# Linear attention and a mixer in one kernel: a new table of ranks and a new order of loads for its planner

## Chip, cores and metric

One core of one Trainium2 chip. The metric is the device time of one execution in microseconds (us). The program computes in fp32 and in pairs of fp32r halves.

## The reference, cut to what matters

```python
# q, k, v: (4, 4, 1088, 32); S1, S2: (8, 32)
def phi(x):                                   # 64 features of a row
    a = einsum('rd,bhsd->bhsr', S1, x)
    b = einsum('rd,bhsd->bhsr', S2, x)
    return einsum('bhsi,bhsj->bhsij', a, b).reshape(*x.shape[:-1], 64)
q_p, k_p = phi(q), phi(k)
kv  = einsum('bhsf,bhsd->bhfd', k_p, v)
z   = sum(k_p, axis=2)
num = einsum('bhsf,bhfd->bhsd', q_p, kv)
den = einsum('bhsf,bhf->bhs', q_p, z)[..., None] + 1e-06
x   = num / den                               # then (4, 1088, 128)
h   = maximum(x.transpose(0, 2, 1) @ w_tok1, 0) @ w_tok2      # 1088 -> 256 -> 1088
u   = x + h.transpose(0, 2, 1)
out = u + maximum(u @ w_ch1, 0) @ w_ch2                       # 128 -> 1536 -> 128
```

The weights arrive as 64-bit floats.

## The kernel before

The work goes batch by batch (b = 0 to 3). For each batch: the features of the keys (`keys`: L534 projects, L564 multiplies, L581 sums them with the values into `kv`, and L591 copies `kv` into the image `kvz`, step `K0.kvz` for batch 0); the features of the queries (for batch 0 on TensorE, L672; for the others `Q1.p` and so on, L727, whose result L736 copies and DMAs turn); then `mixing`: the attention (L790, steps `A0.x0` to `x2`), the denominators (L798) and the division (L806 and L808, steps `A0.d0` to `d2`), token mixing in three groups (L846 for batch 0, L852 for the others, steps `A0.t0` to `t2`), relu, a transpose (L886), the second token matrix (L968, L972) on top of the residual (L877, steps `A0.u0` to `u2`), and the split of the sum into two halves (L943, L946). `channel_mix` takes the columns in spans of 384 (two of 320, one of 256 at the end): for each of 12 slices of the 1536 channels three matmuls L1022 into `ps_h` (steps `.f`), the relu half L1026 on ScalarE (`.h`), the rest L1029 on VectorE (`.l`), and three matmuls L1035 into `ps_o` (`.s`). For the three spans of batch 0 the slices interleave: slices 0 to 2 of the first and of the second span, 3 to 5 of both, 6 to 11 of both, then the third.

A weight piece wi (w = 0, 1 token matrices, 2, 3 channel matrices; "14" is piece 4 of matrix 1) is loaded as doubles and converted by `convert`: `abs` (L384) and `low` (L388) on ScalarE, `clamp` (L391), `shift` (L395, into a `ps_h` bank) and `merge` (L398) on VectorE, `add` (L405, L407) on GpSimd; then `hi` (L504) on ScalarE and `lo` (L507) split it. Pieces 00 to 03 and all of matrices 2 and 3 have 512 columns, 04 has 256, 10 to 13 have 384, 14 and 15 have 320; at 128 partitions and 8 bytes that is 512, 256, 384 and 320 KB (of 1,024 bytes). One batch of keys is 576 KB, of queries 544, of values 594. Of batch 0, the first four key tiles (256 KB) go over ScalarE's queue and k0 is the other 320 KB; q0a is 192 KB and q0b 352.

The program is not written out in its order. Each step is an `Op` with a cost on each engine that may do it, and `Plan.run` places them one by one: of all ready steps it takes those that can start first by its own costs, and of these the one with the highest rank. The rank is the longest chain of costs behind the step plus an offset from the table `LEAD` (in the planner's ns; steps of one name share it). An offset beyond some hundred thousand puts a step before or behind all others that are ready with it. `LOADS` is the order of the loads in SP's queue. Buffers are few: three PSUM banks `ps_a`, three `ps_h`, two `ps_o`; four buffers `c` and four `tail` for conversions. In its own clock the planner keeps VectorE's `port=True` steps and all GpSimd steps from overlapping. Where TensorE would stand idle, `fill` puts matmuls on the identity (L362).

```python
for op in self.ops:
    op.level += op.boost + LEAD.get(op.name, 0.0)
...
first = min(b[0] for b in best)
near = [b for b in best if b[0] <= first]
top = max(near, key=lambda b: b[3].level + STICK * (b[2] == "pe" and b[3].mode == mode))
```

Of the kernel before, what the change touches and what calls it, by code (L numbers as in the profile page):

```python
# [32 lines left out]
PAD = 64  # L33
CUTS = {0: (2, 2, 2, 2, 1), 2: (4, 4, 4), 3: (4, 4, 4)}
SIZES = ([n * DTOK for n in CUTS[0]], [cn for _, cn in CHUNKS for _ in range(2)], [n * P for n in CUTS[2]], [n * P for n in CUTS[3]])
LOADS = "k0 q0a 00 v0 q0b 01 02 03 04 10 k1 11 12 13 q1 20 32 30 21 v1 31 15 22 14".split()


WIDE = 384
# [2 lines left out]
def _spans():  # L42
# [22 lines left out]
KEYS_ON_POOL = set()  # L65

LEAD = {
    "A0.d1": -168600.0,
    "A0.d2": -1620100.0,
    "A0.t2": -90600.0,  # L70
    "A0.u0": -461300.0,
    "A0.u1": 126500.0,
    "A0.ul00": 26500.0,
    "A1.n1": 207400.0,
    "A1.xT0": -108100.0,
    "A2.h0": -154900.0,
    "A2.n0": 210600.0,
    "A2.w1": -3726400.0,
    "A2.w2": -80800.0,
    "A2.x": -16100.0,  # L80
    "A2.xb": -788400.0,
    "A3.n0": 775400.0,
    "A3.n1": 210300.0,
    "A3.w1": 89200.0,
    "A3.w2": 127600.0,
    "K0.kvz": -2428600.0,
    "K1.c0": 982200.0,
    "K1.kvz": -2006700.0,
    "K1.s": -439400.0,
    "K1.v0": 26700.0,  # L90
    "K1.v4": -1229500.0,
    "K2.p": 5500.0,
    "K2.s": 631300.0,
    "K3.p": 645000.0,
    "Q0.a20": 606400.0,
    "Q0.m20": -56700.0,
    "Q0.p1": 183300.0,
    "Q1.r00": 75800.0,
    "Q1.r01": 221700.0,
    "Q1.r11": -287800.0,  # L100
    "Q3.p": -1564300.0,
    "U0.l": -3600.0,
    "U0.s": -888200.0,
    "U1.ol": 570300.0,
    "U1.s": -310000.0,
    "U10.s": -2000.0,
    "U11.s": -1400.0,
    "U2.f": 181200.0,
    "U2.h": -146700.0,
    "U2.s": -764700.0,  # L110
    "U3.f": 8400.0,
    "U3.s": 5700.0,
    "U4.f": 762600.0,
    "U4.h": 68000.0,
    "U6.s": -230900.0,
    "U8.f": 192500.0,
    "U8.s": -591000.0,
    "U9.f": -390200.0,
    "U9.h": 261700.0,
    "s.low": 6600.0,  # L120
    "s.rows": 95400.0,
    "w00.clamp": -462300.0,
    "w00.lo": -3161100.0,
    "w01.abs": 311700.0,
    "w01.hi": -124600.0,
    "w01.lo": -2636700.0,
    "w02.abs": 28200.0,
    "w02.hi": -455000.0,
    "w02.lo": -4313300.0,
    "w02.low": -1051800.0,  # L130
    "w02.shift": 141200.0,
    "w03.clamp": 120200.0,
    "w03.hi": -107500.0,
    "w03.lo": -2645500.0,
    "w03.shift": -1556200.0,
    "w04.hi": -2453000.0,
    "w04.lo": -2852800.0,
    "w10.abs": -1284500.0,
    "w10.clamp": 69000.0,
    "w11.clamp": 246000.0,  # L140
    "w11.hi": -1243300.0,
    "w11.lo": -134000.0,
    "w11.low": 448400.0,
    "w11.merge": -659300.0,
    "w12.abs": 99900.0,
    "w12.hi": 475400.0,
    "w12.low": -24500.0,
    "w12.merge": -269500.0,
    "w13.hi": -300400.0,
    "w13.merge": -144100.0,  # L150
    "w13.shift": -1219700.0,
    "w14.abs": -2780200.0,
    "w14.clamp": 192400.0,
    "w15.abs": -4153500.0,
    "w15.clamp": 149200.0,
    "w20.clamp": -574900.0,
    "w20.low": -1570500.0,
    "w21.low": 310000.0,
    "w22.abs": -997600.0,
    "w22.low": -1298000.0,  # L160
    "w32.abs": -2006300.0,
    "w32.low": -2863700.0,
}


# [154 lines left out]
def attn_mixer_kernel(ctx: ExitStack, tc: tile.TileContext, qT, kT, v1, s64, wt1, wt2, wc1, wc2, out):  # L320
# [143 lines left out]
    by_kind = {"q": (load_q, q_loaded), "k": (load_k, k_loaded), "v": (load_v, v_loaded)}  # L464
    for name in LOADS:
        if name[:2] == "q0":
# [45 lines left out]

    for name in LOADS:
        if name[0].isdigit():
# [566 lines left out]
    for b in range(B):  # L1081
# [3 lines left out]
        if not b:  # L1085

            for name in LOADS:
                if name[0] in "01":
# [58 lines left out]
```

## Time and profile before

| | us |
|---|---|
| median of 3 runs | 220.97 (220.74 to 222.49) |
| the profiled execution | 220.62 |
| its span | 218.7 |
| TensorE's matmuls busy | 211.2 |
| VectorE, ScalarE, GpSimd busy | 137.7, 117.3, 80.3 |

The span runs from the first to the last instruction of the program in the trace. PE is TensorE's matmul, PEld its weight load, DVE VectorE, ACT ScalarE, POOL GpSimd, SP the queue of DMAs. Matmuls are pipelined: their listed durations overlap, so a group's length is read from its start to the next start.

### The profile page before, as it was taken

The page shows a single profiled execution, that of the slowest core. Times are in us where ns is not written, and L with a number is a line of the kernel's source. Part 1 is how long each engine was busy: PE and PEld are TensorE (multiplying, and loading weights), DVE is VectorE, ACT ScalarE, POOL GpSimd, SP SyncE. Part 2 cuts the span into 40 slices and gives each one's busy share as a digit, 9 for nine tenths or more (in the row PEclk, how much of TensorE's full clock was granted, in tenths as well). Part 3 has the DMA queues.
Part 4 walks back from the last instruction along what each step waited for, and adds up shares of the span by engine and source line. Part 5 has one row for each costly group of instructions (what it writes and reads, how often), then busy time and mean ns, then how long its engine had stood idle before and what let it go on. Part 6 is the DMA issues. An engine that isn't in the chain of part 4 may idle for free.

```text
span 218.7 us, 4927 instructions
## 1 busy us (share of the span) xinstructions
PE 211.2 (97%) x1884; PEld 199.4 (91%) x1884; DVE 137.7 (63%) x276; ACT 117.3 (54%) x283; POOL 80.3 (37%) x87
## 2 busy tenths in 40 slices
PE   7997999998999999999999999999999999999994
PEld 7766679997998999999999999999999999999993
DVE  2887999879759456555833455568137655556562
ACT  4588799994545324543532544455226544355551
POOL 3165597989899102740500220745003200000000
PEclk9999999999999999999999999999999999999998
DMA  6999996994106589610250258400510000100000
GB/s 194 390 410 407 406 393 205 186 211 151 37 3 226 128 223 155 172 66 3 85 170 0 74 142 146 174 0 27 191 38 1 3 36 0 36 3 36 0 30 27
DMA packets 11399, 28.36 MB, mean 130 GB/s; under 512 B 1520, under 2 KB 5616, under 8 KB 11376
## 3 DMA queue, kind: packets, MB, share of 16 engines
q1 hardware_dynamic: 11232, 27.79, 41.3%
q8 instruction: 15, 0.25, 0.5%
q10 hardware_dynamic: 144, 0.26, 0.4%
q14 instruction: 8, 0.07, 0.1%
HBM read 23.21 MB, written 4.83 MB: 128 GB/s over the span
## 4 chain that ended last, share of the span: by engine, by line
PE 83%; DMA 11%; DVE 1%; SPq 1%; issue 1%; ACT 0%
PE ps_h L1022 33%; PE ps_o L1035 32%; DMA doubles<-wt 11%; PE ps_a L852 4%; PE ps_a L972 4%; PE ps_a L790 3%; PE ps_a L581 3%; PE ps_a L968 1%; PE ps_a L534 1%; SPq L366 1%; PE ps_a L727 1%; DVE k_p L564 1%; PE ps_a L877 0%; PE ps_a L886 0%; DVE hl L1029 0%
## 5 line engine op out<-in xcount | busy, mean ns | idle before, releaser
L1029 DVE SCALAR_TENSOR_TENSOR hl<-ps_h,hh 128x384 fp32r<-128x384 f32 (+2 forms) x144 | 74.9, 532 | 54.9 <-ACT hh L1026 54.5
L1026 ACT ACTIVATE hh<-ps_h 128x384 fp32r<-128x384 f32 (+2 forms) x144 | 67.8, 477 | 58.7 <-PE ps_o L1035 36.2
L1022 PE MATMUL ps_h<-uh,halves 128*128 128x384 f32 (+2 forms) x288 | 88.1, 334 | 0.9 <-DVE hl L1029 0.9
L1035 PE MATMUL ps_o<-hh,halves 128*128 128x384 f32 (+2 forms) x288 | 70.6, 327 | 0.0
L1022 PEld LDWEIGHTS ps_h<-uh,halves 128*128 128x128 f32 x288 | 53.3, 188 | 4.0 <-DVE hl L1029 2.7
L1035 PEld LDWEIGHTS ps_o<-hh,halves 128*128 128x128 f32 x288 | 50.3, 188 | 0.0
L1022 PE MATMUL ps_h<-ul,halves 128*128 128x384 f32 (+2 forms) x144 | 47.0, 327 | 0.0
L1035 PE MATMUL ps_o<-hl,halves 128*128 128x384 f32 (+2 forms) x144 | 47.0, 327 | 0.0
L1022 PEld LDWEIGHTS ps_h<-ul,halves 128*128 128x128 f32 x144 | 27.1, 188 | 0.2
L1035 PEld LDWEIGHTS ps_o<-hl,halves 128*128 128x128 f32 x144 | 27.0, 188 | 0.0
L946 POOL TENSOR_TENSOR ul<-us,uh 128x64 fp32r<-128x64 f32 (+4 forms) x15 | 9.6, 656 | 46.5 <-ACT uh L943 46.3
L770 POOL TENSOR_TENSOR qp<-qp,br 128x544 f32<-128x544 f32 x12 | 16.2, 1367 | 13.2 <-PE ps_o L1035 9.7
L818 POOL TENSOR_TENSOR xl<-x,xh 128x384 fp32r<-128x384 f32 x9 | 8.9, 1014 | 13.5 <-ACT xh L814 8.5
L564 DVE TENSOR_TENSOR k_p<-ps_a,a_sb 128x1024 f32<-128x1024 f32 (+1 forms) x12 | 11.0, 948 | 4.3 <-ACT a_sb L544 4.3
L405 POOL TENSOR_TENSOR whole<-c,tail 128x512 int32<-128x512 int32 (+3 forms) x11 | 11.7, 1071 | 3.3 <-ACT abT L736 2.0
L384 ACT ACTIVATE c<-doubles 128x512 f32<-128x512 f32 (+3 forms) x17 | 10.7, 628 | 3.2 <-DMA doubles<-wt 2.2
L507 POOL TENSOR_TENSOR halves<-whole,halves 128x384 fp32r<-128x384 f32 (+3 forms) x11 | 11.5, 1062 | 0.0
L790 PEld LDWEIGHTS ps_a<-kvz,qp 128*64 128x64 f32 x288 | 8.8, 138 | 2.5 <-ACT kvz L591 1.3
L790 PE MATMUL ps_a<-kvz,qp 128*64 128x66 f32 x288 | 9.5, 224 | 1.4 <-ACT kvz L591 1.1
L388 ACT ACTIVATE tail<-doubles 128x512 int32<-128x512 uint32 (+3 forms) x17 | 10.5, 624 | 0.0
L395 DVE TENSOR_SCALAR ps_h<-c 128x512 int32<-128x512 int32 (+3 forms) x17 | 10.3, 617 | 0.1
L398 DVE SCALAR_TENSOR_TENSOR c<-doubles,ps_h 128x512 int32<-128x512 int32 (+3 forms) x17 | 10.3, 609 | 0.1
(78 smaller groups left out, 229.0 us busy)
## 6 DMA issues: line engine op xcount, KB each, us to landing
qp<-rows SPq DMA_DIRECT2D x6, 544.0 KB
br<-rows SPq DMA_DIRECT2D x12, 272.0 KB
doubles<-wc SPq DMA_DIRECT2D x6, 512.0 KB
v_sb<-v SPq DMA_DIRECT2D x4, 594.0 KB
doubles<-wt SPq DMA_DIRECT2D x4, 512.0 KB
k_sb<-kT SPq DMA_DIRECT2D x3, 576.0 KB
xm<-xb SPq DMA_DIRECT2D x3, 576.0 KB
xT<-xm SPq DMA_DIRECT2D x12, 144.0 KB
```

Of the source, the lines that this page charges most:

```text
L384: nc.scalar.activation(f32(t["c"]), f32(high), AF.Abs)
L388: nc.scalar.activation(t["tail"], low.bitcast(U32), AF.Copy, scale=2.0 ** -29)
L395: nc.vector.tensor_scalar(t["ps"], t["c"], 3, 0x3FFFFFFF, op0=ALU.logical_shift_left, op1=ALU.bitwise_and)
L405: engines[e].tensor_tensor(dst(), t["c"], t["tail"], op=ALU.add)
L507: engines[e].tensor_tensor(halves[w, i][:, 1], f32(whole[w, i] if w < 2 else t["c"]), f32(halves[w, i][:, 0]), op=ALU.subtract)
L564: engines["pool" if on_pool else "dve"].tensor_tensor(t["k_p"][:pn, t0 * H:t1 * H], a.unsqueeze(3).broadcast_to([pn, n, R, R]), t["sb", t0 ...
L770: engines[e].tensor_tensor(qp[:, p, cs], qp[:, p, cs], t["br"][:, p, cs], op=ALU.mult)
L790: nc.tensor.matmul(x_ps[c:c + 64, o:o + 2 * (D + 1)], lhsT=qp[:, p, s0 + c:s0 + c + 64], rhs=kvz_all[b % 2][:, p, :2 * (D + 1)], start=Tru ...
L1022: nc.tensor.matmul(h_ps[:, :cn], lhsT=part(2, at[2][e][0], l, at[2][e][1] * P, P), rhs=r[:, :cn], start=(m == 0), stop=(m == 2))
L1026: nc.scalar.activation(t["hh"][:, :cn], t["h"][:, :cn], AF.Relu)
L1029: nc.vector.scalar_tensor_tensor(t["hl"][:, :cn], t["h"][:, :cn], 0.0, f32(t["hh"][:, :cn]), op0=ALU.max, op1=ALU.subtract)
L1035: nc.tensor.matmul(outs[i][:, :cn], lhsT=part(3, at[3][e][0], l, at[3][e][1] * P, P), rhs=r[:, :cn], start=(e == 0 and m == 0), stop=(e == ...
```

## The change

Only two tables differ: the order of the loads, and the offsets of the ranks (95 entries before, 93 after). The new ones come from a search over replays of the kernel in which the port shared by VectorE and GpSimd goes to the engine that asked first. Steps, costs, buffers and the planner's rules stay. The diff, cut to the entries that the text speaks of:

```diff
-LOADS = "k0 q0a 00 v0 q0b 01 02 03 04 10 k1 11 12 13 q1 20 32 30 21 v1 31 15 22 14".split()
+LOADS = "00 q0a q0b v0 k0 02 01 03 04 10 q1 11 13 k1 12 20 22 30 31 21 32 15 14 v1".split()
...
 LEAD = {
-    "A0.d1": -168600.0,
-    "A0.d2": -1620100.0,
-    "A0.t2": -90600.0,
-    "A0.u0": -461300.0,
-    "A0.u1": 126500.0,
...
-    "K0.kvz": -2428600.0,
-    "K1.c0": 982200.0,
...
-    "w14.abs": -2780200.0,
-    "w14.clamp": 192400.0,
-    "w15.abs": -4153500.0,
-    "w15.clamp": 149200.0,
...
+    "A0.d0": -218900.0,
+    "A0.d1": -1259700.0,
+    "A0.d2": -2992700.0,
+    "A0.u0": -332800.0,
+    "A0.u2": 6400.0,
...
+    "K0.kvz": -4274900.0,
...
+    "Q1.p": 134300.0,
...
+    "w14.low": 943100.0,
+    "w15.abs": -3839900.0,
+    "w15.clamp": 146300.0,
...
 }
```

## Rows read from the trace of the kernel before

**Rows 1.** The page: busy time of each engine, and the chain that ended last.
```profile
PE 211.2 (97%) x1884; PEld 199.4 (91%) x1884; DVE 137.7 (63%) x276; ACT 117.3 (54%) x283; POOL 80.3 (37%) x87
...
PE 83%; DMA 11%; DVE 1%; SPq 1%; issue 1%; ACT 0%
```
**Rows 2.** Busy time by stretch: PE, PEld, DVE, ACT, POOL; clock, DMA share, GB/s.
```profile
12.00:20.00 8.00, 6.57 (x114) 5.39 (x114) 6.60 (x15) 6.92 (x19) 3.95 (x5) 1.00 1.03 406
20.00:32.00 12.00, 11.44 (x107) 8.29 (x101) 11.79 (x28) 10.01 (x24) 9.18 (x9) 1.00 1.03 404
32.00:54.00 22.00, 21.08 (x176) 19.61 (x175) 19.59 (x35) 19.25 (x44) 20.16 (x18) 1.00 0.79 200
54.00:215.50 161.50, 161.48 (x1375) 157.53 (x1373) 93.02 (x187) 74.55 (x182) 43.38 (x46) 1.00 0.27 75
215.50:218.70 3.20, 0.00 (x0) 0.00 (x0) 0.42 (x1) 0.00 (x0) 0.00 (x0) 0.79 0.12 41
```
**Rows 3.** The chain in order of time, one piece: start, us, what.
```profile
163.07 0.52 PE ps_h L1022 x3
```
**Rows 4.** TensorE in order of time to 34 us: start, us, instructions, idle before.
```profile
4.65 1.75 PE L534 MATMUL ps_a<-s_blocks,k_sb 128*64 128x64 f32 x36
...
12.07 0.80 PE L581 MATMUL ps_o<-v_sb,k_p 128*64 128x66 f32 x20
...
17.43 1.74 PE L790 MATMUL ps_a<-kvz,qp 128*64 128x66 f32 x52 [1.11 <-ACT kvz L591]
...
21.63 0.83 PE L362 MATMUL ps_o<-ident 128*128 128x128 f32 x6
22.58 1.56 PE L846 MATMUL ps_a<-whole,x 128*128 128x256 f32 x6
24.07 0.82 PE L727 MATMUL ps_a<-q_sb,s_rows 64*32 64x272 f32 x16
24.82 1.56 PE L846 MATMUL ps_a<-whole,x 128*128 128x256 f32 x6
...
30.45 0.55 PE L877 MATMUL ps_a<-ident,x 128*128 128x128 f32 x3 [0.15 <-DVE k_p L564]
...
31.83 0.63 PE L1022 MATMUL ps_h<-uh,halves 128*128 128x384 f32 x1
```
**Rows 5.** ScalarE in order of time, 5 to 20 us.
```profile
7.27 0.67 ACT L384 ACTIVATE c<-doubles 128x512 f32<-128x512 f32 x1 [0.46 <-DMA doubles<-wt]
...
10.97 0.68 ACT L384 ACTIVATE c<-doubles 128x512 f32<-128x512 f32 x1 [1.06 <-DMA doubles<-wt]
...
14.72 0.69 ACT L384 ACTIVATE c<-doubles 128x512 f32<-128x512 f32 x1 [0.70 <-DMA doubles<-wt]
...
16.96 0.42 ACT L591 COPY kvz<-ps_o 64x66 f32<-64x66 f32 x2
```
**Rows 6.** VectorE in order of time, 0 to 30 us.
```profile
14.70 0.69 DVE L395 TENSOR_SCALAR ps_h<-c 128x512 int32<-128x512 int32 x1
...
19.99 0.68 DVE L398 SCALAR_TENSOR_TENSOR c<-doubles,ps_h 128x512 int32<-128x512 int32 x1
...
21.97 0.56 DVE L808 TENSOR_TENSOR x<-ps_a,rec 128x384 f32<-128x384 f32 x1
```
**Rows 7.** The weight load that waited for v0, and v's size from the DMA issues.
```profile
8.91 1.60 PEld L581 LDWEIGHTS ps_o<-v_sb,k_p 128*64 128x64 f32 x52 [0.54 <-DMA v_sb<-v]
...
v_sb<-v SPq DMA_DIRECT2D x4, 594.0 KB
```
**Rows 8.** Around the hole at 52 us, in order of time on VectorE, GpSimd and TensorE.
```profile
39.86 0.82 DVE L391 TENSOR_SCALAR c<-c 128x512 f32<-128x512 f32 x1
...
50.75 1.95 DVE L391 TENSOR_SCALAR c<-c 128x320 f32<-128x320 f32 x2
51.14 1.37 POOL L507 TENSOR_TENSOR halves<-c,halves 128x512 fp32r<-128x512 f32 x1
52.62 1.01 DVE L1029 SCALAR_TENSOR_TENSOR hl<-ps_h,hh 128x384 fp32r<-128x384 f32 x2
53.22 0.44 PE L1022 MATMUL ps_h<-uh,halves 128*128 128x384 f32 x1 [0.90 <-DVE hl L1029]
```
**Rows 9.** Line L391 alone: durations in ns, least, median, most.
```profile
L391 DVE TENSOR_SCALAR c<-c x17: 288/419/1410, 8.7 to 51.3; 128x512 f32<-128x512 f32 x10, 128x384 f32<-128x384 f32 x4, 128x320 f32<-128x320 f32 x2, 128x256 f32<-128x256 f32 x1
```

More of the change, by code (lines that the diff above doesn't have):

```diff
@@ L67 @@
 LEAD = {
-    "A0.d1": -168600.0,
-    "A0.d2": -1620100.0,
-    "A0.t2": -90600.0,
-    "A0.u0": -461300.0,
-    "A0.u1": 126500.0,
[L73 to L85, printed above, removed]
-    "K0.kvz": -2428600.0,
-    "K1.c0": 982200.0,
@@ L88 @@
[L88 to L148, printed above, removed]
@@ L149 @@
-    "w13.hi": -300400.0,
-    "w13.merge": -144100.0,
-    "w13.shift": -1219700.0,
-    "w14.abs": -2780200.0,
-    "w14.clamp": 192400.0,
-    "w15.abs": -4153500.0,
-    "w15.clamp": 149200.0,
[L156 to L162, printed above, removed]
+    "A0.d0": -218900.0,
[3 more added lines that the diff above has]
+    "A0.u2": 6400.0,
@@ new lines @@
+    "A0.uh11": 195400.0,
+    "A1.n1": -1088700.0,
+    "A1.t1": -31400.0,
+    "A1.xT0": -344700.0,
+    "A1.xT2": 58400.0,
+    "A1.xT3": 189100.0,
+    "A2.n0": 73400.0,
+    "A2.uh06": 373600.0,
+    "A2.w1": -3374800.0,
+    "A3.h0": -88300.0,
+    "A3.n0": 149500.0,
+    "A3.t0": -280200.0,
+    "A3.uh110": 391700.0,
+    "K0.kvz": -4274900.0,
+    "K1.c8": -97900.0,
+    "K1.kvz": -1122600.0,
+    "K1.v4": -754100.0,
+    "K2.s": 111900.0,
+    "K3.p": 443800.0,
+    "K3.s": -152600.0,
+    "Q0.a01": 42200.0,
@@ new lines @@
+    "Q0.a10": -431500.0,
+    "Q0.a20": -373500.0,
+    "Q0.a21": -635800.0,
+    "Q0.b01": 87200.0,
+    "Q0.b21": -656900.0,
+    "Q0.p2": -1247700.0,
+    "Q1.p": 134300.0,
+    "Q1.r01": -288800.0,
+    "Q2.p": -183100.0,
+    "Q3.p": -999500.0,
+    "U0.h": 148500.0,
+    "U0.l": -137000.0,
+    "U0.s": -299400.0,
+    "U1.f": 619700.0,
+    "U1.l": -318600.0,
+    "U1.oh": 1400.0,
+    "U1.s": -295000.0,
+    "U11.f": 600.0,
+    "U2.s": -713900.0,
+    "U3.h": -584700.0,
+    "U3.s": -58000.0,
@@ new lines @@
+    "U4.f": 147300.0,
+    "U5.s": -140300.0,
+    "U6.f": 55900.0,
+    "U6.s": -129900.0,
+    "U7.s": -947100.0,
+    "U8.s": -283400.0,
+    "U9.h": 132800.0,
+    "s.low": 149300.0,
+    "w00.hi": -728600.0,
+    "w00.lo": -1396500.0,
+    "w00.low": 47100.0,
+    "w01.lo": -3190700.0,
+    "w01.low": -1532000.0,
+    "w02.lo": -4617800.0,
+    "w03.clamp": 226300.0,
+    "w03.hi": -199000.0,
+    "w03.lo": -1658700.0,
+    "w03.shift": 590500.0,
+    "w04.hi": -2521300.0,
+    "w10.clamp": 378100.0,
@@ new lines @@
+    "w10.hi": 42800.0,
+    "w10.shift": -1045900.0,
+    "w11.hi": -576700.0,
+    "w11.lo": -415600.0,
+    "w11.merge": -102500.0,
+    "w12.hi": -281000.0,
+    "w12.low": -298600.0,
+    "w12.shift": -363500.0,
+    "w13.abs": -162800.0,
+    "w13.clamp": 26300.0,
+    "w13.hi": 1010700.0,
+    "w14.low": 943100.0,
+    "w15.abs": -3839900.0,
+    "w15.clamp": 146300.0,
+    "w15.low": -201400.0,
+    "w20.abs": -145800.0,
+    "w21.abs": 28600.0,
+    "w21.lo": -33800.0,
+    "w21.merge": -272700.0,
@@ L163 @@
+    "w22.low": -782800.0,
+    "w30.hi": 47700.0,
+    "w30.shift": -468100.0,
+    "w31.abs": 115200.0,
+    "w31.low": -78800.0,
+    "w32.clamp": -183300.0,
+    "w32.low": -2619000.0,
 }
```

## Prediction

> **What bounds the kernel now.** I read the page's busy shares first, then the chain of work that ended last, then the stretches, then TensorE's instructions in order of time up to 34 us.
>
> TensorE is busy 97% of the span and is 83% of the chain; nothing else has more than the 11% of the weight transfers [rows 1]. The stretches divide the kernel in three [rows 2]. From 54 to 215.5 us TensorE is busy 161.48 of 161.5 us, and three matmuls of 384 columns take 0.52 us [rows 3]: that is a constant stream, and no order of the other engines makes it shorter. After the last matmul 3.2 us remain for the last addition and its transfer; they do not change. What an order can change lies before 54 us. From 32 to 54 us TensorE is busy 21.08 of 22, so about 0.9 us is a real hole. Before 32 us the busy share deceives: L362 is the warm-up and filler matmul on the identity, and it is part of it. Take the useful groups of that view from start to the start of what follows (or, before a hole, their busy time): 36 matmuls of L534 from 4.65, 20 of L581 from 12.07, and so on to the L877 and L968 pair at 30.45, 17 such groups before the first channel matmul (L1022) at 31.83 [rows 4]. They come to about 20.0 us. So of the 27.2 us between 4.65 and 31.83 some 7.2 us are fillers and holes, and the time is set there by something else. With the 0.9 us behind, a new order has about 8 us in all to win, and can lose without such a limit.
>
> What sets the start of the stream is one chain: the image copy L591 (`K0.kvz`), the attention matmuls L790, the division L808, three groups of L846, relu and transpose, L968, the split, L1022. It runs from 16.96 us [rows 5] to 31.83. Its holes are visible. TensorE waits 1.11 us for L591 at 17.43. It waits from 21.63 to 22.58 under fillers for the second L808, which starts only at 21.97, and, between its second and third L846 group (22.58, 24.82), it runs L727, the projection of batch 1 (`Q1.p`), at 24.07 [rows 4, 6]. VectorE is busy 11.79 of 12 us from 20 to 32, ScalarE 10.01 [rows 2]: while the chain waits, they convert weights.
>
> **The change part by part.** No instruction is added or removed; the planned steps keep their durations, and only the planner's choice among ready steps differs. So each term is a wait moved, and I bound each by the hole that it touches.
>
> *Loads.* Up to the fifth name the two lists hold the same loads (k0, q0a, 00, v0, q0b), so the end of that block does not move. The first weight piece comes first: before it stood behind 4 + 256 + 320 + 192 KB, now behind 4 + 256 (partitions x columns x bytes of the code; the profile has 594 KB for v0 by the same count [rows 7]). Before, its conversion began at 7.27 [rows 5] and v0 was awaited until 8.91, 594 KB later [rows 7]: 362 KB per us. 512 KB fewer ahead is 1.4 us sooner, about 5.9 us. The rest of the first keys (k0, 320 KB) goes from first to last: 352 KB behind the old place of v0, about 9.9 us. Their products then end about 12.5, their sums about 14, and L591 could run there; before it ran at 16.96 although the last sums (L581 at 12.07) ended near 12.8 [rows 4, 5]. So the late keys cost nothing while 2 us of cover last; without the cover they cost what exceeds it. What the sooner piece gives: ScalarE waited 0.46, 1.06 and 0.70 us for weights before 15 us [rows 5], and POOL is busy 3.95 of the 8 us from 12 to 20 [rows 2], so holes exist to fill; but pieces 01 to 04 land as a block at the same time as before (01 and 02 change places). Bounds: nothing gained, or the whole 1.4 us. I take -0.3, near the lower end, because the division and not the weights ends the wait at 22.58.
>
> *`Q1.p`.* q1 moves ahead of k1, 11, 12, 13: 1,728 KB fewer ahead of it. At 406 GB/s from the stretch 12 to 20 us [rows 2], that is 396 KB per us, so 4.4 us sooner, and its rank rises by 134,300 with that of the third L846 group (`A0.t2`) back from -90,600. It can then run in filler time before 22 us instead of inside the chain. There it costs 24.82 - 24.07 = 0.75 us. Bounds: 0 to -0.75; I take -0.5.
>
> *The divisions.* `A0.d0` gets -218,900 where it had nothing; `A0.d1` and `A0.d2` fall further, but they already stood behind everything. So d0 alone can newly be passed over by a ready conversion step; the longest are shift and merge, 0.68 us each for 512 columns [rows 6]. VectorE is busy 6.60 of the 8 us before 20 [rows 2], so little can stand ready ahead of it. Bounds 0 to +1.36 (both); I take +0.2.
>
> *`K1.c0`* loses +982,200, the top rank, and k1 lands 1,312 KB, 3.3 us, later. It held two of the three `ps_a` banks: TensorE waited 0.15 us at 30.45 for the first product of batch 1 to free one for the second residual [rows 4]. Later copies free it later, and the second span of the channel stream needs it. The cover is what TensorE has by then: three L1022 groups and three L1035 groups, 6 x 0.52 = 3.1 us [rows 3]; the sums of batch 1 wait for the same products. Bounds: 0, or one and a half conversion pairs of 2 x 0.67 us on ScalarE [rows 5] that go ahead of the copies, +2.0; I take +0.2.
>
> *The hole at 52 us.* The clamps of pieces 14 and 15 (L391, 320 columns) together span 1.95 us, the second 1.41 of it; the median clamp, of 512 columns, takes 0.42 [rows 8, 9]. Behind them in VectorE's order stands the next L1029, which TensorE needs: it waits 0.90 us [rows 8]. The second clamp asked at 51.29, inside a GpSimd subtraction from 51.14 to 52.51. The new ranks separate the two: w14.abs comes back from -2,780,200 to none, so its clamp is ready much sooner, and w14.clamp falls from +192,400 to none; w15.abs stays at the bottom. One clamp near a busy GpSimd is left. A wait of 0.4 us at 39.86 (0.82 us instead of 0.42) left no hole in TensorE [rows 8, 9]. Bounds: 0, or the hole, 0.90; I take -0.7.
>
> On this the Trainium skill, "SBUF — State Buffer", section "SBUF: two separate sides", says that VectorE and GpSimd share one pair of ports as an exclusive lock: whichever starts first keeps it for its whole instruction and the other is blocked. The rows agree: the clamp lasts until 52.70, 0.19 us after that subtraction's end [rows 8]. But the rule speaks against the change: a rank shortens no GpSimd instruction, and by it a clamp anywhere in this stretch, where GpSimd is busy 20.16 of 22 us [rows 2], is likely to wait again; by the rule alone the last term would be near 0.
>
> *Everything else* (the other conversions' ranks, pieces 22, 31, 32, 21, v1): piece 20 and piece 30, which the stream needs first, land at the same KB count as before (20 after 7,190, 30 after 8,214). 32 lands 2,048 KB later but serves the last third of the channels; v1 is now the last load, 1,664 KB or 4.2 us later, and serves the sums of batch 1. I take 0, bounds -0.5 to +0.5, from the other small holes of 32 to 54 us.
>
> Sum: -0.3 - 0.5 + 0.2 + 0.2 - 0.7 = -1.1 us. The profiled execution took 220.62 us, 1.9 more than its span of 218.7. Its span becomes 217.6, its time 219.5; the median shown is 220.97, 0.35 above, so the forecast is 219.9 us.
>
> **The rivals.**
> Bigger gain: the chain's holes close too. If L591 comes 1.4 us sooner with the sooner piece and the 0.75 and 0.90 us go entirely, nothing lost: -3.05, 217.9 us. For it: TensorE's 7.2 us of fillers. Against: VectorE is full from 20 us on.
>
> The clamp waits again (the page's rule as a mechanism of this kernel): the hole only moves. The sum is then -0.4, 220.6 us. For it: GpSimd's load; against: the wait at 39.86 left no hole [rows 8].
>
> Slower: `ps_a` is taken. `Q1.p`, now ahead, holds two of three banks until ScalarE has copied them, and its copies rank behind the conversions. The attention matmuls of the second third and the L846 sum need banks. If it runs before 19.5 us with ScalarE full (6.92 of 8 us from 12 to 20), the second L790 group waits; from about 0.6 us of such wait it eats the whole gain, and two conversion pairs on ScalarE ahead of the copies (four steps of about 0.67 us [rows 5]) make +2.6 instead of -0.5. Sum +2.0, 223.0 us; with `K1.c0` at its bound 224.8.
>
> **How the numbers follow.** Forecast (218.9 to 220.3) 0.35; bigger gain 0.24; clamp again or no change (220.3 to 221.8) 0.22; slower 0.19, of which about two thirds beyond 1%. About 1%, 2.2 us, is what a measurement of this kernel tells from no change. So faster (under 218.8) 0.24, within 0.63, slower (over 223.2) 0.13. The range leaves about one in ten on each side: from 217.2, the bigger gain with a little more of the 7.2 us, to 223.4, between the two prices of the slower case.
>
> **What would show it.** Right: first L384 at about 5.9 us; L727 before the first L846 group; the first L1022 at 31 us or before; no TensorE wait for L1029 around 52; clamps of pieces 14 and 15 apart. Wrong: L790 waiting on a copy of L736; the second L1022 span waiting for the second residual; a clamp over 1 us followed by a TensorE wait; the first L1022 after 32.5.

## The result, and the profile after

| | before | after |
|---|---|---|
| median of 6 executions, us | 220.86 (220.53 to 222.49) | 218.81 (218.47 to 219.25) |
| the profiled execution: time, span | 220.62, 218.7 | 219.25, 217.2 |

The ratio is 0.9895, 95% interval 0.9863 to 0.9927: 2.05 us less by the medians, 1.5 us between the two profiled spans (the profiled execution of after is the slowest of its six). The forecast was 219.9, 1.1 us less. Line numbers of after are 2 smaller than those of before: L1020 is L1022, L389 is L391, L725 is L727.

The page of after, busy time and chain, beside [rows 1]:

```profile
PE 210.7 (97%) x1876; PEld 198.9 (92%) x1876; DVE 137.2 (63%) x276; ACT 117.9 (54%) x284; POOL 79.6 (37%) x86
...
PE 85%; DVE 5%; DMA 5%; SPq 2%; issue 1%; ACT 0%; DVEq 0%
```

The same stretches as [rows 2], PE first (PE, PEld, DVE, ACT, POOL; clock, DMA share, GB/s):

```profile
12.00:20.00 8.00, 6.65 (x128) 5.44 (x129) 7.26 (x18) 7.01 (x19) 3.37 (x4) 1.00 1.03 407
20.00:32.00 12.00, 11.60 (x115) 8.04 (x111) 11.79 (x26) 9.96 (x24) 9.55 (x9) 1.00 1.03 404
32.00:54.00 22.00, 22.00 (x184) 20.89 (x183) 19.87 (x38) 19.38 (x45) 19.89 (x18) 1.00 0.69 195
```

From 32 to 54 us TensorE is now busy 22.00 of 22 where it was 21.08. Before 32 us little moved: TensorE has 11.60 of 12 us where it had 11.44, and VectorE is full again (11.79 of 12). TensorE's starts, beside [rows 4]:

```profile
9.62 0.80 PE L532 MATMUL ps_a<-s_blocks,k_sb 128*64 128x64 f32 x20
...
17.33 1.86 PE L788 MATMUL ps_a<-kvz,qp 128*64 128x66 f32 x48 [1.20 <-ACT kvz L589]
...
20.94 2.76 PE L844 MATMUL ps_a<-whole,x 128*128 128x256 f32 x12
23.63 1.21 PE L725 MATMUL ps_a<-q_sb,s_rows 64*32 64x272 f32 x16
24.77 1.56 PE L844 MATMUL ps_a<-whole,x 128*128 128x256 f32 x6
...
30.87 1.56 PE L966 MATMUL ps_a<-whole,hTl 128*128 128x384 f32 x4
31.97 0.63 PE L1020 MATMUL ps_h<-uh,halves 128*128 128x384 f32 x1
```

The channel stream starts at 31.97, in before at 31.83: no sooner. L725 (`Q1.p`) still stands between the second and the third group of L844. The last matmul starts at 213.72, in before at 215.20. So all of the 1.5 us lies inside the stream, which goes from 183.37 to 181.75 us.

Where it lies is seen in the distance from each matmul's start to the next, less the median distance of its kind. A hole is counted together with the slow matmul right behind it, and what both kernels have alike where TensorE changes from one operation to another is left out. In before four holes stand out: 1.18 us at 52 (of which [rows 8] list 0.90 as idle), and 0.29 at 42.0, 0.25 at 47.6, 0.27 at 89.7. The matmul rows list no idle time at the three small ones; in before the rows of the weight loads do:

```profile
42.36 0.19 PEld L1022 LDWEIGHTS ps_h<-uh,halves 128*128 128x128 f32 x1 [0.28 <-DVE hl L1029]
...
47.88 0.19 PEld L1022 LDWEIGHTS ps_h<-uh,halves 128*128 128x128 f32 x1 [0.29 <-DVE hl L1029]
...
90.01 0.19 PEld L1022 LDWEIGHTS ps_h<-uh,halves 128*128 128x128 f32 x1 [0.32 <-DVE hl L1029]
```

In after there are 0.09 at 42.3 and 0.27 at 51.7. The difference is 1.6 us, 0.9 from the large hole and 0.7 from the small ones. All holes named here but the 0.09 end 0.05 to 0.06 us behind an L1029 (L1027 in after) on VectorE.

The clamps of the pieces 14 and 15 (VectorE and GpSimd of after, in order of time), beside [rows 8]:

```profile
45.16 0.65 DVE L389 TENSOR_SCALAR c<-c 128x320 f32<-128x320 f32 x2
...
46.12 0.74 POOL L505 TENSOR_TENSOR halves<-whole,halves 128x256 fp32r<-128x256 f32 x1 [0.90 <-ACT halves L502]
...
51.63 1.28 POOL L505 TENSOR_TENSOR halves<-c,halves 128x512 fp32r<-128x512 f32 x1
52.37 0.73 DVE L389 TENSOR_SCALAR c<-c 128x320 f32<-128x320 f32 x1
```

The group at 45.16 is the clamps of the pieces 14 and 32, for the most part in a gap of GpSimd of 0.90 us that ends at 46.12; that of piece 15 follows 7 us later. It too asks during a GpSimd subtraction and ends behind it, but late in it, and takes 0.73 us, not 1.41; a clamp of this size that waits for nothing takes 0.32.

### The profile page after: what moved, and what is told of

It reads as the page before. It is cut to its first block, busy times and chain, and to the rows that moved or that the text cites. A ratio compares the mean times of both kernels' runs of the same rounds, so it can differ in the third digit from the quotient of the medians.

```text
span 217.2 us, 4920 instructions
## 1 busy us (share of the span) xinstructions
PE 210.7 (97%) x1876; PEld 198.9 (92%) x1876; DVE 137.2 (63%) x276; ACT 117.9 (54%) x284; POOL 79.6 (37%) x86
## 4 chain that ended last, share of the span: by engine, by line
PE 85%; DVE 5%; DMA 5%; SPq 2%; issue 1%; ACT 0%; DVEq 0%
PE ps_h L1020 34%; PE ps_o L1033 33%; DMA doubles<-wt 5%; PE ps_a L850 4%; PE ps_a L970 4%; PE ps_a L788 4%; PE ps_a L579 3%; SPq L364 2%; DVE c L396 1%; PE ps_a L966 1%; DVE ps_h L393 1%; PE ps_a L532 1%; DVE x L806 1%; DVE c L389 1%; PE ps_a L725 1%
## 5 line engine op out<-in xcount | busy, mean ns | idle before, releaser
L1027 DVE SCALAR_TENSOR_TENSOR hl<-ps_h,hh 128x384 fp32r<-128x384 f32 (+2 forms) x144 | 74.6, 533 | 58.5 <-ACT hh L1024 58.1
L1020 PE MATMUL ps_h<-uh,halves 128*128 128x384 f32 (+2 forms) x288 | 86.6, 332 | 0.0
L1020 PEld LDWEIGHTS ps_h<-uh,halves 128*128 128x128 f32 x288 | 53.1, 188 | 2.2 <-ACT kvz L589 0.4
L1020 PE MATMUL ps_h<-ul,halves 128*128 128x384 f32 (+2 forms) x144 | 47.0, 327 | 0.0
L1020 PEld LDWEIGHTS ps_h<-ul,halves 128*128 128x128 f32 x144 | 27.1, 188 | 0.2
```

The source lines that it names most:

```text
L1020: nc.tensor.matmul(h_ps[:, :cn], lhsT=part(2, at[2][e][0], l, at[2][e][1] * P, P), rhs=r[:, :cn], start=(m == 0), stop=(m == 2))
L1027: nc.vector.scalar_tensor_tensor(t["hl"][:, :cn], t["h"][:, :cn], 0.0, f32(t["hh"][:, :cn]), op0=ALU.max, op1=ALU.subtract)
```

## Experiments

In these kernels the order of all steps on all queues is written out, as before or after has it, and not planned. The diffs are cut to the main step; where other steps move with it, the text says so, and all the rest keeps its place. Lines are numbered as in before (b_psum15: 2 to 3 more, a_psum and a_both: up to 5 more). Each ratio is to before, on the same chip; the runs are spread over several chips, so two runs are compared by their ratios and by their traces rather than by their times.

Several begin with the same program up to the attention and still differ there, so their starts are best compared in two parts (us; read from the traces):

| | attention starts | first channel matmul | between | last matmul starts |
|---|---|---|---|---|
| before | 17.43 | 31.83 | 14.40 | 215.20 |
| b_apart, b_psum15 | 17.20, 17.44 | 31.65, 31.88 | 14.45, 14.44 | 214.51, 214.32 |
| after | 17.33 | 31.97 | 14.64 | 213.72 |
| a_pair, a_d | 16.66, 16.70 | 31.30, 31.28 | 14.64, 14.58 | 214.73, 212.96 |
| a_q | 17.11 | 31.73 | 14.62 | 216.71 |
| a_w | 17.07 | 30.97 | 13.90 | 217.38 |
| a_psum | 16.92 | 31.34 | 14.42 | 213.09 |
| a_kvz, a_both | 16.69, 15.96 | 31.86, 30.93 | 15.17, 14.97 | 213.59, 212.64 |

### One table at a time

**loads_only**: the order of before, the loads of after.

```diff
-LOADS = "k0 q0a 00 v0 q0b 01 02 03 04 10 k1 11 12 13 q1 20 32 30 21 v1 31 15 22 14".split()
+LOADS = "00 q0a q0b v0 k0 02 01 03 04 10 q1 11 13 k1 12 20 22 30 31 21 32 15 14 v1".split()
```

> The kernel before with every engine's order kept as it was; only the 24 loads in SP's queue stand in the new order. Theory A (the gain of the change lies in the order of the work on VectorE, ScalarE and GpSimd around 42 to 52 us): no gain, 220.9 us within 0.7, the first channel matmul (L1022) at 31.8 within 0.4, TensorE's wait of 0.9 us at 52 still there. Theory B (the gain comes from the loads, through an earlier start of what follows them): 219.3 or less.

Measured: 226.11 us, ratio 1.0231 (1.0203 to 1.0259). Both theories fall. TensorE and ScalarE in order of time:

```profile
4.69 1.12 PE L534 MATMUL ps_a<-s_blocks,k_sb 128*64 128x64 f32 x16
9.10 0.87 PE L534 MATMUL ps_a<-s_blocks,k_sb 128*64 128x64 f32 x20 [3.29 <-DMA k_sb<-kT]
9.90 2.08 PE L362 MATMUL ps_o<-ident 128*128 128x128 f32 x8
...
10.02 0.35 ACT L544 COPY a_sb<-ps_a 128x128 f32<-128x128 f32 x2 [3.90 <-PE ps_a L534]
```

In the order of before the second projection of the keys (`K0.p4`) stands ahead of that of the queries. It now waits for k0 until 9.10. TensorE waits 3.29 us, ScalarE 3.90 behind it with the first weight piece in hand, and the first channel matmul comes at 36.13. That is 4.3 us later than in before, more than the wait. TensorE stood still up to 9.10, and its granted clock behind the wait was 0.59 on average, so mostly at the lower of its two levels (1.2 GHz), where before has 1.00 (PE; clock, DMA share, GB/s):

```profile
9.10:12.40 3.30, 3.30 (x30) 0.59 1.02 413
```

Eight fillers L362 took 2.08 us there and 1.16 in before. From the channel matmuls on the stream is that of before, with its large hole (at 56.28).

**loads_p4**: the same, with this one step behind the queries and the first sum; its copies on ScalarE, its products on VectorE and the second projection of the queries move with it.

```diff
 TensorE: K0.p0
-K0.p4
 Q0.p0, K0.s00
+K0.p4
 Q0.p1, K0.s04 ...
```

> The orders of the kernel before with the new order of loads, as in the run loads_only (226.1 us, first channel matmul at 36.1), and with one thing more: the second projection of batch 0's keys (K0.p4), which needs the load k0 that now comes last of the first block, goes behind the first projection of the queries and the first sum (Q0.p0, K0.s00), with its copies, products and the sums that read them. Theory P (this one step is what the new order of loads needs): the wait of TensorE for the keys at 9 us is hidden, ScalarE's conversions are no longer held up, first channel matmul at 31.8 to 32.8, time 220.5 to 221.8, within 0.4% of before. Theory R (many of the new ranks are needed, not one): first channel matmul still after 34, time over 223.

Measured: 220.70 us, ratio 0.9999 (0.9984 to 1.0015); theory P.

```profile
9.72 0.80 PE L534 MATMUL ps_a<-s_blocks,k_sb 128*64 128x64 f32 x20
...
32.19 0.63 PE L1022 MATMUL ps_h<-uh,halves 128*128 128x384 f32 x1
```

The place of one step on TensorE, with what hangs on it, is worth more than 5 us (2.3% between the two ratios), and with it the new loads bring nothing.

**order_only**: the order of after, the loads of before.

```diff
-LOADS = "00 q0a q0b v0 k0 02 01 03 ..."
+LOADS = "k0 q0a 00 v0 q0b 01 02 03 ..."
```

> The changed kernel with every engine's order kept, but its loads in the order of before. Theory A: 218.8 us within 0.7, as the changed kernel; the conversions that were ordered for the new arrivals (02 before 01, 22 before 30) may wait a little for the old ones. Theory B: the gain is gone, 220.5 or more.

Measured: 220.63 us, ratio 0.9986 (0.9971 to 1.0001). ScalarE, and the first channel matmul:

```profile
12.38 0.70 ACT L384 ACTIVATE c<-doubles 128x512 f32<-128x512 f32 x1 [1.54 <-DMA doubles<-wt]
...
32.65 0.63 PE L1022 MATMUL ps_h<-uh,halves 128*128 128x384 f32 x1
```

By its number this is theory B, but loads_p4 doesn't gain by the loads either. The order of after converts piece 02 second; in the old list it stands behind 01, and ScalarE waits 1.54 us for it. The large hole is gone, but the start is late and three small holes stand in the stream (0.30 us at 33.1, 0.23 at 37.3, 0.37 at 43.4). The first ends behind the low half of a weight piece on GpSimd (L507), the other two behind an L1029; why these came late stays open. Neither table gains alone, both together 2 us.

### The hole at 52 us

**b_apart**: the order of before with the two clamps apart.

```diff
 VectorE: w14.clamp
-w15.clamp
 ... w14.shift ... w14.merge
+w15.clamp
```

> The kernel before with one step moved: the clamp of piece 15 goes from right behind the clamp of piece 14 to behind the merge of piece 14, that is behind three L1029 on VectorE. Theory P (the hole at 52 us is the wait of that clamp for GpSimd, in front of an L1029 that TensorE needs): the hole of 0.9 us closes, 220.0 us within 0.4, and the clamp may still be long where GpSimd is busy. Rival (a clamp next to a busy GpSimd delays whatever L1029 stands behind it): the hole moves some us on and keeps 0.5 us or more, 220.6 or more.

Measured: 220.24 us, ratio 0.9973 (0.9959 to 0.9988), span 218.0. GpSimd, VectorE and TensorE:

```profile
53.29 1.01 POOL L507 TENSOR_TENSOR halves<-whole,halves 128x384 fp32r<-128x384 f32 x1
...
53.41 1.07 DVE L391 TENSOR_SCALAR c<-c 128x320 f32<-128x320 f32 x1
...
55.52 0.45 PE L1022 MATMUL ps_h<-uh,halves 128*128 128x384 f32 x1 [0.27 <-DVE hl L1029]
```

The hole at 52 is gone, but the moved clamp asks 0.12 us into the next subtraction, ends 0.18 us after it, and makes a hole of 0.54 us (0.43 and a slow matmul) of its own. The time is what theory P expected, the new hole what the rival did. Apart alone isn't the cure; where the clamp falls counts.

**b_psum15**: the order of before; the clamp of piece 15 writes a free `ps_a` bank instead of its own buffer in SBUF.

```diff
-nc.vector.tensor_scalar(f32(t["c"]), f32(t["c"]), LEAST, MOST, ...)
+nc.vector.tensor_scalar(bank("ps_a")[:rows, :n], f32(t["c"]), LEAST, MOST, ...)
```

> The kernel before in its own order; the clamp of piece 15 writes its 320 columns to a free PSUM bank and not to SBUF, so it is no longer an instruction with both ends in SBUF. Theory P (it waits for the port it shares with GpSimd): it takes 0.4 to 0.5 us where it took 1.41, and TensorE's wait at 52 falls from 0.9 to under 0.3, 220.1 us within 0.4. Rival (it is long for another reason, its input or its place): it stays over 1 us and the time at 220.9.

Measured: 219.92 us, ratio 0.9957 (0.9942 to 0.9971), span 217.8.

```profile
51.18 1.39 POOL L510 TENSOR_TENSOR halves<-c,halves 128x512 fp32r<-128x512 f32 x1
...
51.34 0.48 DVE L393 TENSOR_SCALAR ps_a<-c 128x320 f32<-128x320 f32 x1
51.73 1.00 DVE L1032 SCALAR_TENSOR_TENSOR hl<-ps_h,hh 128x384 fp32r<-128x384 f32 x2
...
52.33 0.44 PE L1025 MATMUL ps_h<-uh,halves 128*128 128x384 f32 x1
```

The clamp runs 0.16 us into the same subtraction (0.15 in before) and takes 0.48 us where it took 1.41; L1032 (L1029 in before) starts 0.9 us sooner, and TensorE's hole falls from 1.18 to 0.25 us. So the wait hung on the clamp's target in SBUF: its input, its place and its work are the same, only the target (and with it what the shift behind it reads) was changed. Whether it is the reading or the writing that waited isn't shown.

**a_pair**: the order of after with the two clamps side by side again; shift and merge of piece 14 move back with its clamp.

```diff
 VectorE:
-w14.clamp
 ... U0.l, U0.l, U0.l
+w14.clamp
 w15.clamp
```

> The kernel after the change, with the clamps of the pieces 14 and 15 put side by side again on VectorE (w14.clamp next to w15.clamp, shift and merge of 14 before those of 15), as they stood in the kernel before. If the pair beside a busy GpSimd is what made the hole of 0.9 us in TensorE at 52 us, one clamp of the two takes over 1 us, TensorE waits 0.6 to 1.2 us for a product L1027 (or for the token matmuls of pieces 14 and 15), and the time is 219.4 to 220.0 against 218.8 of after. If the clamps only lay by chance in the place where another wait ended, the time stays within 0.2 of 218.8.

Measured: 220.42 us, ratio 0.9998 (0.9982 to 1.0014).

```profile
51.66 2.15 DVE L391 TENSOR_SCALAR c<-c 128x320 f32<-128x320 f32 x2
...
52.15 1.47 POOL L770 TENSOR_TENSOR qp<-qp,br 128x544 f32<-128x544 f32 x1
...
54.31 0.49 DVE L395 TENSOR_SCALAR ps_h<-c 128x320 int32<-128x320 int32 x1
54.84 0.49 DVE L398 SCALAR_TENSOR_TENSOR c<-doubles,ps_h 128x320 int32<-128x320 int32 x1
55.24 0.55 DVE L1029 SCALAR_TENSOR_TENSOR hl<-ps_h,hh 128x384 fp32r<-128x384 f32 x1
...
55.85 0.45 PE L1022 MATMUL ps_h<-uh,halves 128*128 128x384 f32 x1 [1.08 <-DVE hl L1029]
```

The first clamp waits for one GpSimd instruction, the second for the next (until 53.62), and TensorE loses 1.4 us here. The stream goes from 181.75 us in after to 183.43; the time is 0.4 us beyond what was expected. This is more than the 0.9 us of before, and it isn't the price of the waits alone: shift and merge of piece 14 stand in front of the L1029 that TensorE waits for, 0.49 us each.

### What sets the start of the stream

Theory X is the prediction's: the chain from the copy `kvz` over attention, division and token mixing. Theory Y: the conversions of weights that stand on VectorE and then GpSimd.

**a_d**: third division sooner. **a_q**: `Q1.p` out of the chain. **a_kvz**: the copy sooner.

```diff
 a_d, VectorE:                a_q, TensorE:            a_kvz, ScalarE:
+A0.d2                        -Q1.p                    +K0.kvz
 w10.merge                     A0.t2 ... U0.f x3        w04.abs, w04.low, w10.low
 w11.clamp                    +Q1.p                    -K0.kvz
-A0.d2
```

> The kernel after the change, with one step moved: on VectorE the third division (A0.d2) goes ahead of the merge of piece 10 and the clamp of piece 11, behind which it stood for 1.1 us. In the trace of after, TensorE's Q1.p (L725 there) ran 1.21 us from 23.63 and not 0.82, because its second half needs the ps_a bank that the third division frees at 24.0, and the third L844 group stood behind it until 24.77. Theory X (the chain of attention, division and token mixing alone sets the start of the channel matmuls): division over at about 23.1, third L844 group at about 24.4, first channel matmul at about 31.6 instead of 31.97, time 218.5 against 218.8 of after. Theory Y (the conversion of the pieces 12 and 20 on VectorE and then GpSimd, which ends at 32.05 in after, sets the start): the third L844 group comes 0.35 us sooner, but the first channel matmul stays within 0.1 us of 31.97 or comes later by what the conversions lost, time 218.8 to 219.3.

Measured: 218.53 us, ratio 0.9909 (0.9893 to 0.9926), like after's 0.9895.

```profile
23.00 0.69 PE L727 MATMUL ps_a<-q_sb,s_rows 64*32 64x272 f32 x16
23.62 1.56 PE L846 MATMUL ps_a<-whole,x 128*128 128x256 f32 x6
...
29.68 0.55 PE L877 MATMUL ps_a<-ident,x 128*128 128x128 f32 x3 [0.37 <-DVE k_p L564]
```

L727 takes 0.69 us instead of 1.21: in after its second half had waited for the bank of the third division. The third L846 comes 6.92 us after the attention's start (7.44 in after), yet the channel matmuls come 14.58 after it (14.64): the 0.5 us is lost again, first behind VectorE's products L564. The time is the one that theory X had named, but the ratio is after's, and by the trace it is theory Y.

> The kernel after the change, with Q1.p (the 16 matmuls of 0.82 us that project the queries of batch 1) taken out of the token mixing on TensorE and put behind the third group of channel matmuls, its copies and its four transfers with it. This prices the 0.5 us that the prediction gave to this step. Theory X (the chain sets the start): the third L844 group comes right behind the second at about 24.06, first channel matmul about 31.0 instead of 31.97; the 0.75 us of matmuls then stand in the stream, so the time is 218.6 (-0.2). Theory Y (the conversions set the start): third L844 group at 24.06 too, first channel matmul 31.7 or later, and the time is 219.2 to 219.6, since the 0.75 us is paid in full.

Measured: 221.40 us, ratio 1.0031 (1.0011 to 1.0051). The two copies on ScalarE and the transfers moved with the step, and the load k2 went ahead of them. The start is the same (14.62), so theory Y, and more is paid than the matmuls:

```profile
53.26 1.36 POOL L770 TENSOR_TENSOR qp<-qp,br 128x544 f32<-128x544 f32 x1 [1.43 <-DMA br<-rows]
...
55.98 0.44 PE L1035 MATMUL ps_o<-hh,halves 128*128 128x384 f32 x1 [0.97 <-POOL halves L507]
```

`Q1.p` also starts four transfers. They now land late, the GpSimd product that reads them waits 1.43 us, and the low half of a weight piece behind it in GpSimd's queue makes TensorE lose 1.24 us, counted as the holes above.

> The kernel after the change, with the copy L589 (K0.kvz) moved on ScalarE ahead of the conversion of piece 04. In after the sums that it copies end at about 14.0, the copy stands behind four conversion steps and a wait for a load of 0.47 us, and starts at 16.77; TensorE waits 1.20 us for it. Moved, it fits into that wait and starts at about 15.0. Theory X (the chain that starts at this copy sets the start of the channel matmuls, as the prediction said): attention from about 15.6, channel matmuls 1.2 us or more sooner, time about 217.6. Theory Y (the conversions of weights, which fill VectorE from about 11 us on, set it): the wait of TensorE goes from in front of the attention to behind it, the channel matmuls start at most 0.4 us sooner (VectorE's one hole of 0.48 us at 17.3 closes), time 218.4 to 218.9.

Measured: 218.59 us, ratio 0.9907 (0.9887 to 0.9927).

```profile
16.69 0.92 PE L790 MATMUL ps_a<-kvz,qp 128*64 128x66 f32 x24
18.17 0.92 PE L790 MATMUL ps_a<-kvz,qp 128*64 128x66 f32 x24 [0.56 <-ACT xT L690]
...
20.83 2.76 PE L846 MATMUL ps_a<-whole,x 128*128 128x256 f32 x12
```

The wait in front of the attention is gone and stands inside it; L846 starts at 20.83 (20.94 in after). The keys landed late in this execution (their second projection at 10.30, in after 9.62), so 0.5 us either way can't be read from it; theory X's 1.2 us (217.6 us, a ratio of about 0.984) is excluded by the time.

**a_psum**: after, with the clamps of the pieces 11 and 15 written into PSUM.

```diff
-clamp of w11, w15: c <- c
+clamp of w11: ps_h <- c (the bank that its shift takes anyway)
+clamp of w15: ps_a <- c
```

> The kernel after the change, with the two clamps that still waited beside GpSimd writing into PSUM instead of SBUF: piece 11 (0.78 us at 22.43 in after, into the ps_h bank that its shift takes anyway) and piece 15 (0.73 us at 52.37, into a free ps_a bank, as in the run b_psum15). If the wait is for the port to SBUF, both take about 0.45 us as groups of one, the third division comes 0.3 us sooner, and the small hole of TensorE around 52 (0.16 + 0.11 us) closes. By theory Y VectorE's queue is what counts before 32 us, so the channel matmuls start up to 0.3 us sooner and the time is 218.3 to 218.7; if GpSimd's queue is the limit, only the hole at 52 counts and the time is 218.6 to 218.8.

Measured: 218.66 us, ratio 0.9912 (0.9894 to 0.9931). The clamp of piece 11:

```profile
22.03 0.55 DVE L395 TENSOR_SCALAR ps_h<-c 128x384 f32<-128x384 f32 x1
```

It took 0.78 us in after. VectorE's queue is 0.23 us shorter, and the channel matmuls start 14.42 us after the attention instead of 14.64: of the edits that keep the order of the matmuls this alone, which shortens VectorE's queue, moved them, and by its own size (a_both against a_kvz: 14.97, 15.17). The 0.27 us at 51 us stayed, so it isn't the clamp's: the L1027 that ends it in after had waited 0.86 us for ScalarE.

**a_w**: after, with the conversion of piece 20 ahead of those of 12 and 13, and two groups of channel matmuls ahead of the second residual.

```diff
 VectorE: -w13.merge, w12.shift | w20.merge | +w13.merge, w12.shift
 GpSimd:  +w20.lo | w12.add | -w20.lo;  +w20.add | w13.add | -w20.add
 ScalarE: +w20.hi | K1.c0 to c8 | -w20.hi
 ScalarE: +U0.h, U0.h, A0.uh11 | w21.low, w13.hi ... | -A0.uh11, U0.h, U0.h
 TensorE: -A0.u1, A0.w1 | U0.f, U0.f | +A0.u1, A0.w1 | U0.f
```

> The kernel after the change, with the conversion of piece 20 put ahead of those of pieces 12 and 13 (merge on VectorE, addition and low half on GpSimd, high half on ScalarE ahead of the copies of K1.p), the split of the first residual ahead of the second product of batch 1, and the first two groups of channel matmuls ahead of the second residual and its token matmuls (A0.u1, A0.w1), which need piece 12. Theory Y (conversions set the start): the low half of piece 20 ends at about 30.7 instead of 32.05, the first channel matmul starts at about 31.0, nothing waits behind it, time 218.4 (-0.4). Theory X (the chain sets it): the first channel matmul comes sooner only because A0.w1 is behind it (31.3), and the 1.1 us of A0.w1 and later waits take it back: time 218.8 within 0.2. If GpSimd's whole queue is the limit (piece 12's addition now 0.9 us later), a wait of about 0.3 to 0.9 us comes in front of A0.w1 and the time is 219.0 to 219.5.

Measured: 222.94 us, ratio 1.0115 (1.0087 to 1.0143). None of the three expectations holds. The first channel matmul comes at 30.97 (13.90 after the attention), but then (ScalarE, GpSimd, TensorE):

```profile
34.36 0.48 ACT L943 CAST uh<-ps_a 128x384 fp32r<-128x384 f32 x1 [1.13 <-PE ps_a L968]
...
35.95 1.01 POOL L507 TENSOR_TENSOR halves<-whole,halves 128x384 fp32r<-128x384 f32 x1 [3.70 <-issue]
...
40.02 0.41 PE L1022 MATMUL ps_h<-uh,halves 128*128 128x384 f32 x1 [1.08 <-DVE hl L1029]
```

I had put the second split L943 ahead of all conversions on ScalarE. It waits there for the token matmuls, the cast of piece 13 waits behind it, and GpSimd stands 3.70 us. (On VectorE the low half of the first split also went ahead, and one product of batch 1 back.) The run says nothing on Y; it shows what a step placed too early in an in-order queue costs.

**a_both**: a_kvz and a_psum together.

```diff
+K0.kvz
 w04.abs, w04.low, w10.low
-K0.kvz
-clamp of w11, w15: c <- c
+clamp of w11: ps_h <- c, of w15: ps_a <- c
```

> The two moves on after that lost nothing, together: the copy L589 (K0.kvz) ahead of the conversion of piece 04 on ScalarE, and the clamps of pieces 11 and 15 written into PSUM. If both gains that the traces show in the start add up (0.2 us from the clamp of piece 11, 0 to 0.5 us from VectorE's hole at 17.3 closed by the copy's move), the time is 218.0 to 218.5, ratio to before about 0.988. If the landing of the loads, which shifts the start by up to 0.6 us between executions of the same program, hides them, it is not to be told from after's ratio of 0.9895.

Measured: 218.31 us, ratio 0.9887 (0.9854 to 0.9921), span 216.2. The channel matmuls start at 30.93, but attention too is early in this execution (15.96). It can't be told from after's 0.9895; I claim no better version.

## Why the prediction was right and wrong

The direction and the range were right, the size about half. The measured 218.81 us lies at the edge of the stretch that the prediction gave to the bigger gain, but that rival's mechanism, an earlier start of the stream, did not come about. That the sum is as near as it is has a share of luck: the 0.5 us of `Q1.p` that failed to come and the 0.7 us of small holes that came unforeseen nearly cancel. By its terms:

- **The hole at 52 us (-0.7): right, a little too small.** 0.9 us came back. The rows showed the idle 0.90 us; the distances between starts show 1.18, and 0.27 stayed. The mechanism is shown by b_psum15, which changes the clamp's target alone, and borne out by b_apart and a_pair, which move other steps past it too. The rule weighed against it, "SBUF — State Buffer", section "SBUF: two separate sides", in the Trainium skill, holds in its mechanism: each clamp from SBUF to SBUF that asked well inside a GpSimd instruction ended just behind it (0.18 us in b_apart). By it the wait should have moved rather than gone; in b_apart it did, in after one clamp fell for the most part into a gap of GpSimd and the other asked late in an instruction. Only the order in time of both engines tells which.
- **Everything else (0, bounds -0.5 to +0.5): failed.** The three small holes gave 0.7 us. I had read the idle time of the matmul rows alone; these holes are hidden in the listed durations, as in this group of before, which takes 0.79 us where others of its kind take 0.51. VectorE in front of it:

```profile
40.69 0.56 DVE L1029 SCALAR_TENSOR_TENSOR hl<-ps_h,hh 128x384 fp32r<-128x384 f32 x1
41.17 0.68 DVE L395 TENSOR_SCALAR ps_h<-c 128x512 int32<-128x512 int32 x1
41.76 0.55 DVE L1029 SCALAR_TENSOR_TENSOR hl<-ps_h,hh 128x384 fp32r<-128x384 f32 x1
...
42.01 0.79 PE L1022 MATMUL ps_h<-uh,halves 128*128 128x384 f32 x2
```

VectorE has no break from the clamp at 39.86 [rows 8] to the L1029 that TensorE waits for here. So the premise that this clamp's wait of 0.4 us left no hole doesn't stand: a hole of 0.29 us lies at the end of that queue. In after the same L1027 ends 10.28 us behind the stream's start, not 10.48, and the hole is 0.2 us smaller. Which of the moved steps did this, and what closed the other two, was not tested.

- **Loads (-0.3): near in size, wrong in a premise.** The first conversion of a weight piece ran at 6.05 (forecast 5.9; it is the step `low`, not `abs`), the sums of the keys ended at 13.98 (14). Attention starts at 17.36 on average in the three profiles with before's beginning and at 16.97 in six with after's, 0.4 us sooner; the profiled execution of after was the late one of them. That takes both tables: with one of them attention starts at 17.77 (loads_p4) and 18.02 (order_only). But "the late keys cost nothing while 2 us of cover last" holds only because the new ranks put `K0.p4` behind the queries. I looked for the cover along the products and sums, and not at what stands behind the waiting step in TensorE's own queue: some 5 us in loads_only.
- **`Q1.p` (-0.5): failed twice.** It did not move: it needs two of three `ps_a` banks, and those were held until the second and third division. In "the slower rival" I had named that condition, and not applied it to the term. And the 0.75 us would not have come: a_q takes it out, and the start stays.
- **Divisions (+0.2) and `K1.c0` (+0.2).** Neither is seen as such. The stretch from attention to channel matmuls is 0.2 us longer (14.64 against 14.40 to 14.45): the second token matmuls L966 now start at 30.87, behind the conversion of piece 12 that ends on GpSimd at 30.81.

```profile
29.81 1.00 POOL L403 TENSOR_TENSOR whole<-c,tail 128x384 int32<-128x384 int32 x1
```

In a_d, a_q, a_kvz and a_psum too these matmuls start 0.05 to 0.06 us behind this addition.
- **What sets the start: failed.** "One chain from `kvz` to L1022" was read from TensorE's waits. Three edits that shortened the chain left the start where it was (a_kvz within what its late keys allow); the one that shortened VectorE's queue moved it, and what the token matmuls in front of the stream waited for was a conversion. The row was there: VectorE busy 11.79 of 12 us [rows 2]. The count beside it was off as well: by the same rule the useful groups before 31.83 come to 20.6 us and not 20.0, so fillers and holes to 6.5 and not 7.2; no term of the sum hangs on it.

0.9 and 0.7 in the stream, 0.4 - 0.2 ahead of it: 1.8 of the 2.05 us. The rest is within the intervals. Of this the cause of the 0.9 is shown by experiment; the 0.7 and the 0.2 are located, and their causes argued from the traces.

## What to carry to other kernels

Price a changed order of loads by what stands behind each late load's first reader on its in-order engine, not only by the chain that reads the data. Where an engine is full, a shorter chain elsewhere gains nothing there. A short instruction that waits for another engine's instructions goes into a gap of that engine or gets a target in PSUM, and two of them don't stand side by side. Look for small holes of TensorE from start to start, and in the rows of the weight loads.

## What was new about the hardware

A clamp from SBUF to SBUF that asked early in a GpSimd instruction took until 0.18 us behind its end (1.07 to 1.41 us in all, 0.32 without a wait), and two in a row took until behind two instructions (2.15 us). The same clamp with PSUM as its target took 0.48 us beside a GpSimd subtraction that ran all the while, though its input lay in SBUF. Behind a stand of 3.3 us TensorE's granted clock was 0.59 for the next 3.3 us (loads_only). Runs of one program up to the attention, on several chips, differed there by 0.67 us (16.66 to 17.33).
